# A decode step (attention over a cache, mixed with a gated feed-forward): VectorE's eight groups as a hardware loop, and the result stored over two queues

## The chip, the cores and the metric

The kernel runs on one core of a Trainium2 chip. The metric is the device time of one execution in microseconds (us). A core has TensorE (PE, matrix products), VectorE (DVE), ScalarE (ACT), GpSimd (POOL) and SyncE (SP), each with its own instruction stream, and sixteen DMA engines that all of them share. The streams are tied together by semaphores only: an instruction waits until a semaphore has reached a value, and raises one when it is done.

## What is computed

One token attends to a cache of 32768 positions with 32 query heads and 8 key/value heads, and the result is mixed with a gated feed-forward of the same token.

```python
g = sigmoid((x * gate_w).sum(-1, keepdims=True))
q = (x @ wq) as 32 heads of 128
k, v = the caches, each of 8 heads used by 4 query heads
p = softmax(q . k / sqrt(128), over 32768 positions)
a = (p @ v) as one row of 4096, @ wo           # 4096 x 512
b = (silu(x @ w_gate) * (x @ w_up)) @ w_down   # 512 -> 1792 -> 512
out = g * a + (1 - g) * b                      # 1 x 1 x 512, bf16
```

Each cache has 8 x 32768 x 128 bf16 numbers, 67 MB. Every number of the caches and weights is read once, 148.1 MB in all, and the output is 1 KB.

## The kernel before, in words

**Groups and pages.** A group (`G` = 8) is one key/value head with its four query heads (`HPG`). Its 32768 positions come in two halves (`NB` = 2) of 16384, and one half of K or of V is a page: 128 partitions x 32 KB, 4.19 MB. There are five page buffers: two for K (`PG_K`), two for V (`PG_V`; one of them first holds the gate and up weights) and one that first holds `wq` and later `wo`.

**Loads.** All large loads are issued by SP, in one order written out by hand: `wq`, gate, up, the first K and V pages, then K and V pages in turn, and at the end `wo` in five pieces with `w_down` between (lines 291 to 319). A K page's buffer is loaded again when PE has made the last transposition from it (`sem_fill`, in `load_k`), a V page's when PE's products on it are done (`sem_v_free`). SP issues in order: a load that waits holds up those behind it.

**A K page.** PE transposes it 1024 positions at a time (eight transpositions, line 387, into one of two PSUM buffers `pst`); VectorE copies that to SBUF (`ktT`, four buffers, line 667); PE multiplies the copy by the group's queries (`qcur`, line 399) into `ps_sc`. There are eight such units per page (`UPP`). PE runs two units ahead (`LAG`): its transpositions into a `pst` buffer wait for the copy two units back (`sem_cp`). After each page VectorE takes the maximum over it (line 672), and after both pages the maximum of the two (line 674). GpSimd takes that over the partitions, ScalarE turns it into a bias and computes the exponentials (line 545).

**A V page.** PE multiplies the exponentials with it (line 443). The sums stand in strips of partitions; ScalarE copies them out (`acc`, line 557), and four small products (`emit_reduce`, line 425) gather them in a few columns of `ps_m`, which VectorE copies to `oT` (`copy_red`, line 658).

**Loops.** PE's stream is a hardware loop already: `pe.Fori(0, (G + 1) * STEP, STEP)`, in which turn g does the K pages of group g and the V pages of group g - 1. Its waits compare semaphores with the loop's register `i` plus a constant, which is why several semaphores advance by `STEP` = 16 per group. VectorE, ScalarE, GpSimd and SP have the eight groups written out, each with constant wait values.

**The end.** After the last group VectorE adds the exponentials' sums, takes their reciprocals, scales `oT` (line 695) and transposes it; PE multiplies by `w_down` and `wo`, the first 18 pieces of `wo` as wide rows, the other 14 as four strips (line 466). VectorE copies the four strips to `res_row` (line 705), in partitions 0, 32, 64 and 96. SP, which waits for that (`sem_dve_row`), stores the four rows of 128 with one DMA (line 322) and waits for its completion.

Of the kernel before, what the change touches and what calls it, by code (L numbers as in the profile page):

```python
# [6 lines left out]
ALU = mybir.AluOpType  # L7
AX = mybir.AxisListType
# [5 lines left out]
def bass_gated_mix__gqa_block_cached__swiglu_ffn__decode_kernel(  # L14
# [18 lines left out]
    HPG = H // G  # L33
# [22 lines left out]
    SCALE = float(DH) ** -0.5  # L56
    assert UPG == STEP and UPP % NKT == 0 and UPP % NST == 0
    assert KC * H * DH <= PAGE and 2 * KC * F <= PAGE and WOJ * NOUT <= PAGE
# [15 lines left out]
    with ExitStack() as es:  # L74
# [53 lines left out]
        def T(name, shape, dt):  # L128
            return es.enter_context(nc.sbuf_tensor(name, shape, dt))
# [21 lines left out]
        qT = T("qT", [128, H], BF16)  # L151
        qblk = T("qblk", [128, G, 2, 2 * HPG], BF16)
        qcur = T("qcur", [128, 2, 2 * HPG], BF16)
# [6 lines left out]
        ET = T("ET", [128, NT, HPG], BF16)  # L160
        pmaxf = T("pmaxf", [128, G * NB, HPG], FP32)
        pmax = T("pmax", [128, G, HPG], FP32)
        gmax = T("gmax", [128, G, HPG], FP32)
# [4 lines left out]
        acc = T("acc", [128, RQ, DH], FP32)  # L168
        oT = T("oT", [128, H], FP32)
        rS = T("rS", [128, H], FP32)  # L170
# [30 lines left out]
        wgu = page[:, PG_F, 0 : 2 * KC * F].rearrange("p (w c f) -> p w c f", w=2, c=KC)  # L201
        wo_v = page[:, PG_X, 0 : WOJ * NOUT].rearrange("p (j n) -> p j n", j=WOJ)

        with nc.Block("main") as block:
            @block.gpsimd
            def _(pool):
# [58 lines left out]
                for g in range(G):  # L265
                    pool.wait_ge(sem_pmax, 3 * (g + 1))
                    pool.partition_all_reduce(  # L267
                        gmax[:, g, :], pmax[:, g, :], 128, ReduceOp.max
                    ).then_inc(sem_gmax, 1)

            @block.sync
            def _(sp):
# [46 lines left out]
                for k in range(1, len(sem_wo)):  # L319
                    load_wo(k)  # L320
                sp.wait_ge(sem_dve_row, 1)
                sp.dma_start(
                    out[0, 0, :].rearrange("(c n) -> c n", c=OC),
                    res_row[0 : 32 * (OC - 1) + 1 : 32, :],
                ).then_inc(sem_out, 16)
                sp.wait_ge(sem_out, 16)

            @block.tensor
            def _(pe):
# [78 lines left out]
                def emit_k(i, b):  # L408
                    pe.wait_ge(sem_page[PG_K[b]], i + 16)
                    for u in range(UPP + LAG):  # L410
                        if u >= LAG:
                            pe.wait_ge(sem_cp, i + (UPP * b + u - LAG + 1))
                        if u < UPP:
                            emit_fill(b, u)
                        if u >= LAG:
                            if u == LAG:
                                pe.wait_ge(sem_exp, i + 8 * (b + 1))
                            ins = emit_scores(b, u - LAG)
                    ins.then_inc(sem_sc, 1)

                def emit_reduce(i):
                    pe.wait_ge(sem_acc, i)
                    pe.wait_ge(sem_rc, i)
                    for q in range(RQ):
                        ins = pe.matmul(  # L425
                            ps_m[:, M_P0 : M_P0 + HPG],
                            acc[:, q, :],
                            sel4[:, q * HPG : (q + 1) * HPG],
                            start=(q == 0),
                            stop=(q == RQ - 1),  # L430
                        )
                    ins.then_inc(sem_red, 1)

# [89 lines left out]
            def _(act):  # L523
# [30 lines left out]
                def emit_acc(g):  # L554
                    act.wait_ge(sem_v_free, NB * (g + 1))
                    act.wait_ge(sem_red, g + 1)
                    act.activation(  # L557
                        acc[:, :, :].rearrange("p q d -> p (q d)"), ps_o[:, :], ACT.Copy
                    ).then_inc(sem_acc, STEP)

                for g in range(G):
                    emit_exps(g)
                    if g:
                        emit_acc(g - 1)
                emit_acc(G - 1)

            @block.vector
            def _(dve):
# [7 lines left out]
                dve.memset(acc[:, :, :], 0.0).then_inc(sem_acc, STEP)  # L576
                dchain(dve.memset(qblk[:, :, :, :], 0.0))
                dve.sem_inc(sem_rc, 2 * STEP)
# [44 lines left out]
                for par in range(2):  # L623
                    lo, hi = 64 * par, 64 * (par + 1)
                    dchain(
                        dve.tensor_copy(
                            qblk[lo:hi, :, :, par * HPG : (par + 1) * HPG],
                            ps_o[lo:hi, 0 : 2 * H].rearrange(
                                "p (e g h) -> p g e h", e=2, h=HPG
                            ),  # L630
                        )
                    )
                dve.tensor_copy(qcur[:, :, :], qblk[:, 0, :, :])
                dve.memset(ps_o[:, :], 0.0).then_inc(sem_ps0, 1)
# [20 lines left out]

                def copy_red(g):
                    dve.wait_ge(sem_red, g + 2)
                    dve.tensor_copy(
                        oT[:, g * HPG : (g + 1) * HPG], ps_m[:, M_P0 : M_P0 + HPG]
                    ).then_inc(sem_rc, STEP)  # L660

                for g in range(G):
                    for b in range(NB):
                        f = NB * g + b
                        for u in range(UPP):
                            dve.wait_ge(sem_fill, UPP * f + u + 1)
                            dve.tensor_copy(  # L667
                                ktT[:, u % NKT, :], pst[u % NST][:, :].bitcast(BF16)
                            ).then_inc(sem_cp, 1)
                        dve.wait_ge(sem_sc, f + 1)  # L670
                        sc = ps_sc[b][:, :].rearrange("p (t h) -> p h t", h=HPG)
                        dve.tensor_reduce(pmaxf[:, f, :], sc, AX.X, ALU.max).then_inc(sem_pmax, 1)  # L672
                    dve.wait_ge(sem_pmax, 3 * g + 2)
                    dve.tensor_tensor(  # L674
                        pmax[:, g, :], pmaxf[:, f - 1, :], pmaxf[:, f, :], ALU.max
                    ).then_inc(sem_pmax, 1)
                    if g + 1 < G:
                        dve.tensor_copy(qcur[:, :, :], qblk[:, g + 1, :, :])
                    if g >= 2:
                        copy_red(g - 2)  # L680

# [4 lines left out]
                dve.memset(ps_w[:, :], 0.0).then_inc(sem_psw, 1)  # L686
                copy_red(G - 2)
                dve.wait_ge(sem_pe_S, 1)
# [3 lines left out]
                )  # L692
                copy_red(G - 1)
                dve.wait_ge(sem_rc, STEP * (G + 2))
                dve.tensor_tensor(oTs[:, :], oT[:, :], rSg[:, :], ALU.mult).then_inc(
                    sem_dve_oT1, 1
                )
                dve.wait_ge(sem_dve_oT1, 1)
# [35 lines left out]
```

## Time and profile before

| | |
|---|---|
| time, median of 3 runs | 354.7 us (354.43 to 354.92) |
| the profiled execution's own time | 353.97 us |
| its span (first to last instruction) | 352.2 us |
| PE busy | 266.7 us (76%) |
| VectorE busy, 203 instructions | 177.5 us (50%) |
| ScalarE busy | 32.3 us (9%) |
| GpSimd busy | 5.8 us (2%) |
| DMA | 148.24 MB, mean 421 GB/s |
| mean granted PE clock | 0.849 |

The profile is of one execution. Its page gives each engine's busy time, the span cut into 40 slices with the busy share of each in tenths, the DMA queues, and groups of instructions: line, engine, operation, output<-input with sizes, count, then busy time and mean duration, and after the bar the idle time in front of them and what ended it. A chain of waits follows the work that ended last back from the end, each piece with its start and length. Other answers of the trace are a timeline (start, duration, instruction) and windows (busy time per engine in a stretch with counts, then granted clock, DMA share and GB/s). "SPq" and "ACTq" are the DMA issues of SP and ACT. "issue" is time in which an engine waited for nothing that the profile shows. What lies between the span and the execution's time is before the first or after the last instruction.

### The profile page before, as it was taken

Reading aid. Unit: us, or ns where it says so; the run is one execution under the profiler, and the core shown is the slowest. Engines: PE = TensorE matmul, PEld = TensorE weight load, DVE = VectorE, ACT = ScalarE, POOL = GpSimd, SP = SyncE. Lnnn points to the kernel's source line nnn. Section 1 sums busy time; section 2 is a strip of 40 time slices with the busy share of each in tenths; the row PEclk is TensorE's granted clock in tenths of the full one; section 3 lists DMA queues with packets and bytes.
Section 4 is the critical chain, followed back from the end, with each engine's and each line's share of the span. In section 5 each row is a group of like instructions: output and inputs, shape, how many; then the busy total and the mean of one; then the engine's idle time right before and its main releaser. Section 6 shows DMA issues by size and latency. Waiting matters only on the chain.

```text
span 352.2 us, 8737 instructions
## 1 busy us (share of the span) xinstructions
PE 266.7 (76%) x4005; PEld 227.3 (65%) x4005; DVE 177.5 (50%) x203; ACT 32.3 (9%) x148; POOL 5.8 (2%) x24
## 2 busy tenths in 40 slices
PE   0446996998999959796897969794987849794365
PEld 0436986967796939494886849492967749492122
DVE  0311877644783929275473819183654719292001
ACT  1000000400030040003000040004000120004000
POOL 0200000000000000000000000000000000000000
PEclk9999989876998989679696969789698969899565
DMA  8999999999999999999999999999999999999994
GB/s 328 411 443 422 437 437 423 419 424 447 435 421 424 447 436 417 424 443 443 417 424 435 447 421 424 435 443 424 424 435 443 424 421 435 443 424 412 426 425 170
DMA packets 5925, 148.24 MB, mean 421 GB/s; under 512 B 666, under 2 KB 668, under 8 KB 924
## 3 DMA queue, kind: packets, MB, share of 16 engines
q1 hardware_dynamic: 5912, 148.12, 98.2%
q8 instruction: 6, 0.10, 0.1%
q14 instruction: 3, 0.02, 0.0%
q10 hardware_dynamic: 4, 0.00, 0.0%
HBM read 148.11 MB, written 0.00 MB: 421 GB/s over the span
## 4 chain that ended last, share of the span: by engine, by line
DMA 62%; PE 33%; DVE 3%; SPq 1%; issue 0%
DMA page<-in_A_k_cache_dram 55%; PE pst L387 24%; DMA page<-in_A_wo_dram 7%; PE ps_sc L399 6%; DVE ktT L667 3%; PE ps_o L443 2%; PE pst L466 1%; PE ps_m L425 0%; SPq L293 0%; SPq L310 0%; SPq L316 0%; SPq L291 0%; SPq L274 0%; DVE res_row L705 0%
## 5 line engine op out<-in xcount | busy, mean ns | idle before, releaser
L667 DVE COPY ktT<-pst 128x2048 bf16<-128x2048 bf16 x128 | 155.8, 1224 | 108.5 <-PE pst L387 101.4
L387 PE MATMUL pst<-ident_f,page 128*128 128x128 f32 x1024 | 156.1, 309 | 40.7 <-DMA page<-in_A_k_cache_dram 38.9
L387 PEld LDWEIGHTS pst<-ident_f,page 128*128 128x128 f32 x1024 | 132.5, 160 | 52.2 <-DMA page<-in_A_k_cache_dram 46.9
L399 PE MATMUL ps_sc<-qcur,ktT 128*128 128x8 bf16 x2048 | 67.8, 166 | 8.6 <-DVE ktT L667 8.6
L399 PEld LDWEIGHTS ps_sc<-qcur,ktT 128*128 128x128 bf16 x2048 | 66.9, 97 | 11.3 <-DVE ktT L667 10.0
L443 PE MATMUL ps_o<-page,ET 128*16 128x512 bf16 x512 | 44.3, 507 | 10.0 <-DMA page<-in_A_v_cache_dram 10.0
L443 PEld LDWEIGHTS ps_o<-page,ET 128*16 128x16 bf16 x512 | 13.7, 107 | 30.2 <-issue 24.5
L536 ACT ACTIVATE nbias<-gmax 128x4 f32<-128x4 f32 x8 | 1.7, 206 | 262.1 <-POOL gmax L267 262.1
L545 ACT ACTIVATE ET<-ps_sc,nbias 128x128 bf16<-128x128 f32 x64 | 24.1, 553 | 0.7
L545 ACT ACTIVATION_READ_ACCUMULATOR ET<-ps_sc,nbias 128x1 f32 x64 | 18.0, 282 | 0.0
L672 DVE TENSOR_REDUCE pmaxf<-ps_sc 128x4 f32<-128x512 f32 x16 | 11.1, 692 | 10.4 <-PE ps_sc L399 10.4
L425 PE MATMUL ps_m<-sel,acc 128*128 128x4 f32 x72 | 10.4, 268 | 3.7 <-ACT acc L557 3.7
L425 PEld LDWEIGHTS ps_m<-sel,acc 128*128 128x128 f32 x72 | 9.8, 211 | 4.4 <-ACT acc L557 4.4
L372 PE MATMUL ps_m<-xT,page 128*128 128x1 bf16 x112 | 6.9, 198 | 5.2 <-DMA page<-in_B_w_up_dram 5.2
L372 PEld LDWEIGHTS ps_m<-xT,page 128*128 128x128 bf16 x112 | 6.8, 159 | 5.3 <-DMA page<-in_B_w_up_dram 5.3
L689 DVE RECIPROCAL rS<-pst 128x32 f32<-128x32 f32 x1 | 0.4, 358 | 17.3 <-PE pst L478 17.3
L267 POOL PARTITION_ALL_REDUCE gmax<-pmax x8 | 3.0, 374 | 292.3 <-DVE pmax L674 292.3
L348 PE MATMUL ps_m<-xT,page 128*128 128x1 bf16 x128 | 3.5, 165 | 4.8 <-DMA page<-in_A_wq_dram 4.8
L557 ACT ACTIVATE acc<-ps_o 128x512 f32<-128x512 f32 x8 | 5.2, 648 | 18.3 <-PE ps_o L443 18.3
L348 PEld LDWEIGHTS ps_m<-xT,page 128*128 128x128 bf16 x128 | 3.5, 104 | 4.8 <-issue 4.8
L335 PE MATMUL ps_m<-ones_bf,x_row 1*128 1x1 bf16 x4 | 0.3, 172 | 8.3 <-DMA gw_row<-in_gate_w_dram 8.3
L335 PEld LDWEIGHTS ps_m<-ones_bf,x_row 1*128 1x128 bf16 x4 | 0.2, 114 | 8.3 <-DMA gw_row<-in_gate_w_dram 8.3
(68 smaller groups left out, 27.6 us busy)
## 6 DMA issues: line engine op xcount, KB each, us to landing
page<-in_A_k_cache_dram SPq DMA_DIRECT2D x16, 4096.0 KB, 27.6
page<-in_A_v_cache_dram SPq DMA_DIRECT2D x16, 4096.0 KB, 31.2
page<-in_A_wq_dram SPq DMA_DIRECT2D x1, 4096.0 KB, 12.6
page<-in_A_wo_dram SPq DMA_DIRECT2D x2, 1024.0 KB, 24.8
page<-in_B_w_gate_dram SPq DMA_DIRECT2D x1, 1792.0 KB, 16.5
page<-in_B_w_up_dram SPq DMA_DIRECT2D x1, 1792.0 KB, 21.2
wd<-in_B_w_down_dram SPq DMA_DIRECT2D x1, 1792.0 KB, 21.7
page<-in_A_wo_dram SPq DMA_DIRECT2D x1, 1280.0 KB, 24.3
```

Of the source, the lines that this page charges most:

```text
L267: pool.partition_all_reduce(gmax[:, g, :], pmax[:, g, :], 128, ReduceOp.max).then_inc(sem_gmax, 1)
L348: ins = pe.matmul(ps_m[:, M_Q0 + h : M_Q0 + h + 1], wq_v[:, c, h * DH : (h + 1) * DH], xT[:, c : c + 1], start=(c == 0), stop=(c == KC - 1),)
L372: ins = pe.matmul(ps_m[:, base + j : base + j + 1], wgu[:, w, c, :].rearrange("d (p j) -> d j p", j=FC)[:, j, :], xT[:, c : c + 1], start= ...
L387: ins = pe.transpose(pst[u % NST][:, k * 128 : (k + 1) * 128], kv[:, n * 128 : (n + 1) * 128], ident_f[:, :],)
L399: ins = pe.matmul(ps_sc[b][:, col : col + 2 * HPG], kt[:, k, e, :], qcur[:, e, :], start=(e == 0), stop=(e == 1),)
L425: ins = pe.matmul(ps_m[:, M_P0 : M_P0 + HPG], acc[:, q, :], sel4[:, q * HPG : (q + 1) * HPG], start=(q == 0), stop=(q == RQ - 1),)
L443: ins = pe.matmul(ps_o[32 * c : 32 * c + RQ * HPG, :], ET[:, n : n + RQ, :].rearrange("p n h -> p (n h)"), view[:, k * RQ : (k + 1) * RQ, ...
L466: ins = pe.matmul(ps_c[32 * oc : 32 * oc + 1, 0:128], lhs, rhs[:, oc * 128 : (oc + 1) * 128], start=first, stop=last, skip_group_check=True,)
L545: act.activation(ET[:, b * R : (b + 1) * R, h], sc[:, h, :], ACT.Exp, bias=nbias[:, g, h : h + 1], scale=SCALE, accum_out=esum[:, g, b, h ...
L557: act.activation(acc[:, :, :].rearrange("p q d -> p (q d)"), ps_o[:, :], ACT.Copy).then_inc(sem_acc, STEP)
L667: dve.tensor_copy(ktT[:, u % NKT, :], pst[u % NST][:, :].bitcast(BF16)).then_inc(sem_cp, 1)
L672: dve.tensor_reduce(pmaxf[:, f, :], sc, AX.X, ALU.max).then_inc(sem_pmax, 1)
```

## The change

VectorE's eight groups become one body in a hardware loop whose register `i` runs from 0 in steps of 16. Its waits use `i` plus a constant. The semaphores that VectorE waits for or raises in the loop now advance by 16 per group (`sem_sc` by 8 per page, `sem_pmax` by 4 + 4 + 8, `sem_red` by 16), and PE, ScalarE and GpSimd follow suit in their values. Tiles that are addressed by group are addressed by `i`: `pmax` and `oT` get 16 columns per group of which 4 are used, `oT` with two unused groups in front; `qblk` becomes flat, with two more groups that stay zero, since the copy to `qcur` now also runs after the last group. `pmaxf` has two rows per turn instead of sixteen in all. The copy of the reduced row, which the first two groups don't have, stands behind a test of the register. The store of the result becomes two DMAs of two rows, one issued by SP and one by ScalarE, and SP waits for both.

```diff
-        qblk = T("qblk", [128, G, 2, 2 * HPG], BF16)
+        qblk = T("qblk", [128, (G + 2) * STEP], BF16)
-        pmaxf = T("pmaxf", [128, G * NB, HPG], FP32)
-        pmax = T("pmax", [128, G, HPG], FP32)
+        pmaxf = T("pmaxf", [128, NB, HPG], FP32)
+        pmax = T("pmax", [128, (G + 1) * STEP], FP32)
-        oT = T("oT", [128, H], FP32)
+        oT = T("oT", [128, (G + 2) * STEP], FP32)
...
+        def store(eng, k):
+            eng.dma_start(
+                out[0, 0, 256 * k : 256 * (k + 1)].rearrange("(c n) -> c n", c=2),
+                res_row[64 * k : 64 * k + 33 : 32, :],
+            ).then_inc(sem_out, 16)
...
                 sp.wait_ge(sem_dve_row, 1)
-                sp.dma_start(
-                    out[0, 0, :].rearrange("(c n) -> c n", c=OC),
-                    res_row[0 : 32 * (OC - 1) + 1 : 32, :],
-                ).then_inc(sem_out, 16)
-                sp.wait_ge(sem_out, 16)
+                store(sp, 0)
+                sp.wait_ge(sem_out, 32)
...
                 emit_acc(G - 1)
+                act.wait_ge(sem_dve_row, 1)
+                store(act, 1)
...
-                def copy_red(g):
-                    dve.wait_ge(sem_red, g + 2)
-                    dve.tensor_copy(
-                        oT[:, g * HPG : (g + 1) * HPG], ps_m[:, M_P0 : M_P0 + HPG]
-                    ).then_inc(sem_rc, STEP)
-
-                for g in range(G):
+                def copy_red(i, at):
+                    dve.wait_ge(sem_red, i)
+                    dve.tensor_copy(oT[:, at], ps_m[:, M_P0 : M_P0 + HPG]).then_inc(sem_rc, STEP)
+
+                with dve.Fori(0, G * STEP, STEP) as i:
                     for b in range(NB):
-                        f = NB * g + b
                         for u in range(UPP):
-                            dve.wait_ge(sem_fill, UPP * f + u + 1)
+                            dve.wait_ge(sem_fill, i + (UPP * b + u + 1))
                             dve.tensor_copy(
                                 ktT[:, u % NKT, :], pst[u % NST][:, :].bitcast(BF16)
                             ).then_inc(sem_cp, 1)
-                        dve.wait_ge(sem_sc, f + 1)
+                        dve.wait_ge(sem_sc, i + 8 * (b + 1))
                         sc = ps_sc[b][:, :].rearrange("p (t h) -> p h t", h=HPG)
-                        dve.tensor_reduce(pmaxf[:, f, :], sc, AX.X, ALU.max).then_inc(sem_pmax, 1)
-                    dve.wait_ge(sem_pmax, 3 * g + 2)
+                        dve.tensor_reduce(pmaxf[:, b, :], sc, AX.X, ALU.max).then_inc(sem_pmax, 4)
+                    dve.wait_ge(sem_pmax, i + 8)
                     dve.tensor_tensor(
-                        pmax[:, g, :], pmaxf[:, f - 1, :], pmaxf[:, f, :], ALU.max
-                    ).then_inc(sem_pmax, 1)
-                    if g + 1 < G:
-                        dve.tensor_copy(qcur[:, :, :], qblk[:, g + 1, :, :])
-                    if g >= 2:
-                        copy_red(g - 2)
+                        pmax[:, bass.ds(i, HPG)], pmaxf[:, 0, :], pmaxf[:, 1, :], ALU.max
+                    ).then_inc(sem_pmax, 8)
+                    dve.tensor_copy(
+                        qcur[:, :, :].rearrange("p e n -> p (e n)"), qblk[:, bass.ds(i + STEP, STEP)]
+                    )
+                    with dve.If(i > STEP):
+                        copy_red(i, bass.ds(i, HPG))
...
-                copy_red(G - 2)
+                copy_red(G * STEP, slice(G * STEP, G * STEP + HPG))
...
-                copy_red(G - 1)
+                copy_red((G + 1) * STEP, slice((G + 1) * STEP, (G + 1) * STEP + HPG))
                 dve.wait_ge(sem_rc, STEP * (G + 2))
-                dve.tensor_tensor(oTs[:, :], oT[:, :], rSg[:, :], ALU.mult).then_inc(
-                    sem_dve_oT1, 1
-                )
+                dve.tensor_tensor(
+                    oTs[:, :].rearrange("p (g h) -> p g h", h=HPG),
+                    oT[:, 2 * STEP :].rearrange("p (g s) -> p g s", s=STEP)[:, :, 0:HPG],
+                    rSg[:, :].rearrange("p (g h) -> p g h", h=HPG),
+                    ALU.mult,
+                ).then_inc(sem_dve_oT1, 1)
```

## The prediction, on record before the run

> **What bounds the kernel now.** I read the slices and queues first, to see whether any resource is full from end to end.
>
> ```profile
> DVE  0311877644783929275473819183654719292001
> DMA  8999999999999999999999999999999999999994
> GB/s 328 411 443 422 437 437 423 419 424 447 435 421 424 447 436 417 424 443 443 417 424 435 447 421 424 435 443 424 424 435 443 424 421 435 443 424 412 426 425 170
> q1 hardware_dynamic: 5912, 148.12, 98.2%
> q8 instruction: 6, 0.10, 0.1%
> q14 instruction: 3, 0.02, 0.0%
> ```
>
> The DMA engines are busy in every slice but the first and last; the loads alone take 98.2% of sixteen engines' span. VectorE (DVE) is busy half of the time. So the end is set by 148.12 MB at the DMA rate, with a start and a tail around it. Second, the chain of waits, for what lies after the last byte:
>
> ```profile
> 277.42 28.47 DMA page<-in_A_k_cache_dram
> ...
> 319.76 0.33 SPq L274
> ...
> 321.08 26.38 DMA page<-in_A_wo_dram
> 347.46 0.04 issue
> 347.50 1.88 PE pst L466 x56
> 349.38 0.03 issue
> 349.41 0.41 PE pst L466 x7
> 349.82 0.02 issue
> 349.85 0.29 DVE res_row L705
> ```
>
> A K page lands 28.47 us after its issue, although 4.19 MB at 431 GB/s (the windows row of 122 to 320 us) are 9.7 us: 18.7 us of other loads lie ahead of it. The last 4.7 us (347.50 to 352.19) are final row products, result copy and store. Third, how far SP runs ahead, because a slower VectorE can only matter by delaying the semaphores that release SP's loads. The windows give what had been moved at three issues:
>
> ```profile
> 0.00:44.40 44.40, 22.83 (x402) 22.46 (x403) 13.74 (x34) 1.67 (x3) 2.82 (x16) 1.00 0.97 409
> 0.00:92.75 92.75, 65.06 (x1018) 60.95 (x1019) 45.28 (x63) 6.16 (x21) 3.21 (x17) 0.91 0.99 419
> 0.00:319.76 319.76, 251.66 (x3826) 220.80 (x3826) 174.30 (x192) 28.49 (x131) 5.81 (x24) 0.87 1.00 428
> ```
>
> The last column is GB/s. At 44.40 us (SP's K load after the first page's last transpose), 20.45 MB had been issued (wq and three pages of 4.19 MB, two weights of 1.835 MB) and 44.40 x 409 = 18.16 MB moved: 2.29 MB, or 5.3 us at 431 GB/s, were still queued. At 92.75 us: 41.42 issued, 38.86 moved, 5.9 us left. At 319.76 us: 148.12 less the 9.18 MB issued from there on (V page 4.19, wd 1.84, rest of wo 3.15) is 138.94; 136.86 moved; 4.8 us left. Between 122 and 320 us the queue is deeper, as the 28.47 us show. These three are the thinnest covers.
>
> **The change part by part.**
>
> *Same work, looped.* The eight groups keep their 128 copies, 16 reduces and 8 maxima; one more qcur copy runs after the last group. It takes 0.17 us (row of L678) and lies before a VectorE idle of 3.73 us (until ScalarE's exponentials are done, 322.61). The semaphore steps are rescaled to match on PE, ACT and POOL, with no instruction more or less there: 0. The larger qblk memset (112 ns for 64 columns, 80 now) lies in the first 9 us, before VectorE's 7.30 us wait for PE: 0.
>
> *Register waits.* Before every K copy but the first there is now a register add, since its wait compares with the loop counter plus a constant: 15 to 16 adds a turn. The copies stand here:
>
> ```profile
> L667 DVE COPY ktT<-pst 128x2048 bf16<-128x2048 bf16 x128 | 155.8, 1224 | 108.5 <-PE pst L387 101.4
> 46.25 0.29 issue
> ```
>
> No register add on VectorE is in the trace. Lower bound of its price: 0, because PE already does the same adds between its groups (one before each transposition group of eight), and its chain alternates 0.93 us of L387 with 0.38 us of L399 without a gap. Upper bound: 0.29 us, PE's issue time at 46.25 where it passes the boundary of a K part, branches and an add together. I take 0.03 us: a sequencer can work on the next add while the copy of 1.224 us runs. VectorE's eight copies take 10.20 us, a period of (10.20 - 1.22)/7 = 1.28 us, against PE's 0.93 + 0.38 = 1.31 us per unit, so 0.03 us is all free room there is; any more than that goes into the page's time. What is late next is the last transposition of the page, then SP's K load, then the DMA queue if it runs dry. Up to 92.75 us there are 32 copies. PE waited for DMA in front of two of those pages (2.55 us before 61.92, 1.68 us before 81.38), so lateness is eaten by 4.2 us there. The queue goes dry only if 32d > 4.2 + 5.9, d = 0.32 us per copy. At 44.40 us eight copies give d = 0.66; at 319.76 us the last page waited for its own data at 305.88, so 8d > 4.8, d = 0.60. Even the upper bound of 0.29 us stays below 0.32. Cost: 0; without that cover it would be 128 x 0.03 = 4 us.
>
> *Loop, branch, addresses.* Each turn adds about five control instructions: two for register addresses, the test for the reduced row, the counter add and the branch back. At 0 to 0.29 us each that is 0 to 1.5 us a turn. They stand behind the second reduce, where VectorE waits for PE's next transposes anyway: 3.55 us at 63.93, 1.88 us at 97.49 (the shortest), 4.74 to 8.21 later. The wait for s_pmax now holds the address instruction; behind it are the maximum, the qcur copy, the row copy and the branch. GpSimd's maximum, then the exponentials, then PE's next scores wait for them. In the last group the maximum ends at 318.80 and the V page that needs the exponentials lands only at 325.46; exponentials end at 322.57, so 2.9 us cover it. Cost 0 at either bound.
>
> *Code loading.* The trace has nine instruction packets in the span, while PE's own loop makes nine turns of over 400 matmuls; a loop that loaded its body on every turn could not do with nine. All of them are 0.12 MB, 0.3 us at 431 GB/s, which bounds the gain from a shorter VectorE program: 0 to -0.3 us. I take -0.05, the 0.02 MB of q14. The Trainium skill (Runtime: NRT & Kernel Launch, Instruction fetch mechanics) speaks against the change: a taken branch whose target lies outside the two resident blocks waits for a fetch, and so kernels prefer full unrolling. With the roughly 2 us that DMA: Bandwidth & Descriptors gives as a transfer's fixed cost, eight turns would be an estimate of 16 us of VectorE idle, of which only the excess over each turn's cover could reach the end; the packet count above says the body stays resident.
>
> *Store.* It is on the path:
>
> ```profile
> 0.72 0.51 ACTq L524 DMA_DIRECT2D x_row<-in_A_x_dram  x1
> 1.27 0.21 ACTq L525 DMA_DIRECT2D gw_row<-in_gate_w_dram  x1
> 350.17 0.63 SPq L322 DMA_DIRECT2D out_dram<-res_row  x1
> SPq L204 <- DMA out_dram<-res_row: 1.0, 1, 1.0
> ```
>
> The columns are start, duration, queue and line; the last row is SP's wait. One issue of four rows takes 0.63 us, and 1.0 us more to completion. After, SP and ACT are released by the same semaphore and issue two rows each side by side. ACT has nothing else left (its last copy ends at 341.95). If the shorter transfer issues like SP's page loads (0.33 us), the gain is 0.30 us; if ACT's issue comes wholly behind SP's at its own 0.21 to 0.63 us, the loss is up to 0.63. ACT's first issue took 0.51, its second 0.21, so two issues overlapped are nearest to 0.5 to 0.63: I take 0.
>
> *Tail on VectorE.* Output scaling reads a strided oT of the same 128x32 size (0.19 us). It feeds the wide products, which end at 346.51, and the partial row at 347.25, while the next products wait for wo data until 347.50 and the partial row is used from 348.20: 0.9 us of cover. Cost 0 unless the tile read goes over five times slower.
>
> **Sum.** Span 352.2 + 0 (waits) + 0 (loop) - 0.05 (code) + 0 (store) = 352.15 us. Around the span lie 353.97 - 352.19 = 1.78 us, giving 353.9 for a run like the profiled one. The median of 354.7 is 0.73 us above that execution, so 354.65, written 354.7. The bounds of the unknown parts are -0.3 - 0.3 = -0.6 and +0.63: 354.1 to 355.3. A measurement of this kernel tells about 0.2% (0.71 us) from no change, and its three runs spread over 0.49 us.
>
> **Rivals.**
>
> *Slower: register waits empty the load queue.* Place: the copies of the first four K pages, where PE and VectorE paced each other and the queue held 5 to 6 us. It decides from 0.32 us per copy. At 0.5 us, 32 x 0.5 - 10.1 = 5.9 us of idle DMA engines, and 360.6 us in all. For it: only 0.03 us of room in a unit. Against: it needs more than the largest control price in the trace, sixteen times in a row. Chance 0.09.
>
> *Slower: the two stores follow each other.* If ACT's store starts only when SP's is through (0.63 + 1.0 us), the end is 1.6 us later: 356.3. For it: ACT has issued nothing for 349 us, and the kernel now ends with the later of two. Against: the two queues have no semaphore between them. Chance 0.08.
>
> *Faster: the stream itself gets shorter.* The rate is 431 GB/s between 122 and 320 us, but 409 up to 44.40. If VectorE's code packets cost more than their bytes, and the store gains 0.3, it is 0.3 + 0.3 + some 0.3 = 0.9 us: 353.8. For it: the slower early stretch. Against: q14 is three packets. Chance 0.10.
>
> *The split does nothing.* If the store's time is in its completion alone, the result is the forecast's; it is counted there.
>
> **How the numbers follow.** Forecast (covered everywhere) 0.73; rivals 0.09, 0.08, 0.10. Faster 0.10, same 0.73, slower 0.17. The range goes from 354.0, just outside the lower bound, to 356.3, which takes in the serial stores; left out are the emptied queue (0.09) and most of the faster case (0.09). The likeliest case alone spans 354.1 to 355.3.
>
> **What would show it.** DMA busy 9 in all middle slices and 431 GB/s from 122 to 320 us: waits covered. A copy group of eight at 10.2 to 10.5 us: adds hidden; over 12.8 us (0.32 x 8 more): the first rival. Idle before the first copy of each turn still put down to PE: loop covered. No more than nine instruction packets: body resident. The last result copy within 0.3 us of 349.85, and from its end to the span's end 2.05 us before: over 3 us means the second rival. A span that moves with DMA idle, or an end that is not the store, would make the prediction wrong.

## The result, and the profile after

The changed kernel takes 353.89 us (median of 13 runs, 353.25 to 354.30) against 354.56 us for before in the same comparison (13 runs, 354.15 to 355.00). The ratio is 0.998, with a 95% interval from 0.9972 to 0.9989: faster by 0.2%, which is small, but the interval leaves out 1. The forecast was 354.7 us and no measurable change, with a range from 354.0; the result lies 0.1 us below that range.

The first rows are those shown of before: VectorE's and the DMA engines' slices and three of the DMA queues, from the changed kernel's page. The profiled execution took 353.30 us with a span of 351.5 us (before: 353.97 and 352.2).

```profile
DVE  0311958565692938266563818283655628183011
DMA  8999999999999999999999999999999999999995
q1 hardware_dynamic: 5908, 148.11, 98.4%
q8 instruction: 6, 0.10, 0.1%
q14 instruction: 2, 0.02, 0.0%
```

The loads bound it as before. One line differs: q14 had three instruction packets, and has two. The chain of waits at the end (start, length, what):

```profile
276.27 28.75 DMA page<-in_A_k_cache_dram
...
346.59 0.04 issue
346.64 1.88 PE pst L469 x53
348.51 0.03 issue
348.54 0.41 PE pst L469 x8
348.95 0.02 issue
348.97 0.29 DVE res_row L713
```

Piece for piece it is the chain of before, 0.87 us earlier: the last products start at 346.64 where they started at 347.50, and the result copy at 348.97 where it started at 349.85. So the gain was made in the loads, and some of it is lost behind the copy, in the store. The timeline shows its two issues (start, length, queue), and SP's waits its completion (total, times, longest):

```profile
349.29 0.60 SPq L205 DMA_DIRECT2D out_dram<-res_row  x1
349.30 0.58 ACTq L205 DMA_DIRECT2D out_dram<-res_row  x1
```

```profile
SPq L210 <- DMA out_dram<-res_row: 1.2, 1, 1.2
```

The two issues do run side by side, but one of two rows takes 0.60 us where one of four took 0.63, and the wait behind it is 1.2 us instead of 1.0. From the end of the result copy to the end of the span it is 351.5 - 349.26 = 2.24 us against 352.19 - 350.14 = 2.05.

VectorE's copies as a group, and from the timeline the boundary of two groups:

```profile
L671 DVE COPY ktT<-pst 128x2048 bf16<-128x2048 bf16 x128 | 155.9, 1224 | 106.0 <-PE pst L390 98.9
```

```profile
82.59 10.20 DVE L671 COPY ktT<-pst 128x2048 bf16<-128x2048 bf16 x8 [5.58 <-PE pst L390]
93.50 0.69 DVE L676 TENSOR_REDUCE pmaxf<-ps_sc 128x4 f32<-128x512 f32 x1 [0.72 <-PE ps_sc L402]
94.33 0.16 DVE L678 TENSOR_TENSOR pmax<-pmaxf 128x4 f32 x1
94.44 0.17 DVE L681 COPY qcur<-qblk 128x16 bf16 x1
96.29 10.20 DVE L671 COPY ktT<-pst 128x2048 bf16<-128x2048 bf16 x8 [1.68 <-PE pst L390]
```

A copy takes 1224 ns and eight of them 10.20 us, both as before: the register adds are hidden. The same boundary before:

```profile
94.63 0.69 DVE L672 TENSOR_REDUCE pmaxf<-ps_sc 128x4 f32<-128x512 f32 x1 [0.65 <-PE ps_sc L399]
95.36 0.16 DVE L674 TENSOR_TENSOR pmax<-pmaxf 128x4 f32<-128x4 f32 x1
```

The wait in front of a reduce grew from 0.65 to 0.72 us, and between the reduce and the maximum there are 0.14 us (94.33 - 94.19) where there were 0.04. The idle time before the next group is still put down to PE.

**Where the load time went.** The loads have the same bytes and the same sum of packet times in both traces (345.63 and 345.65 us per engine, from the start, length and size of each packet), yet the last byte lands at 349.26 us before and at 348.38 us after. (Times of packets are counted here and below so that the first load packet starts at 2.10 us in every run; on the span's own clock, which the fences use, they are 0.33 to 0.37 us smaller.) The sixteen engines don't finish together, and the kernel waits for the last. Each engine has the same series of packet sizes, so the trace's packets can be strung into sixteen series by size and by start behind the end of the one before. Two engines that run in step can be taken for each other, but the sixteen end times hold. Sorted, in us:

```
before   346.4 346.5 346.7 346.8 346.8 346.9 347.2 347.2 348.0 348.1 348.1 348.2 348.2 348.2 348.3 349.26
changed  346.5 346.6 346.6 346.7 346.8 346.9 347.4 347.7 348.0 348.0 348.1 348.1 348.2 348.2 348.4 348.38
```

(The last two of the changed kernel are 348.35 and 348.38.) Six engines end near 346.5, some at 348 or a little more, and in before one is a microsecond behind all others. The packets between the loads explain the steps: a 16 KB instruction packet (q8, all between 19 and 66 us) stands about 1.0 us in an engine's line, and the load packet behind it mostly takes some 0.5 us longer than the usual 1.22 us; an 8 KB one (q14) stands 0.3 us and lengthens the next by 0.25 to 0.65 us. Before had 8 KB packets at 59.5, 131.4 and 285.4 us, the changed kernel at 59.7 and 131.3. The one at 285.4 us stood 0.33 us, and the load packet that starts at its end took 1.87 us: 0.98 us for that engine, and the last engine ends 0.95 us behind the next. So the first theory (F in the expectations): the packet at 285.4 us was VectorE's code, it fell on an engine that was late already, and the shorter program doesn't need it. The trace doesn't name a packet's engine, so that it was the late one is argued from the end times.

### The profile page after: what moved, and what is told of

Read it like the earlier page. It is cut to its first block, busy times and chain, and to the rows that moved or that the text cites. A ratio compares the mean times of both kernels' runs of the same rounds, so it can differ in the third digit from the quotient of the medians.

```text
span 351.5 us, 8924 instructions
## 1 busy us (share of the span) xinstructions
PE 263.6 (75%) x4005; PEld 228.2 (65%) x4005; DVE 178.6 (51%) x204; ACT 32.1 (9%) x148; POOL 5.8 (2%) x24
## 4 chain that ended last, share of the span: by engine, by line
DMA 61%; PE 33%; DVE 3%; SPq 1%; issue 1%
DMA page<-in_A_k_cache_dram 54%; PE pst L390 24%; DMA page<-in_A_wo_dram 7%; PE ps_sc L402 6%; DVE ktT L671 3%; PE ps_o L446 2%; PE pst L469 1%; PE ps_m L428 0%; SPq L299 0%; SPq L316 0%; SPq L322 0%; SPq L297 0%; SPq L280 0%; DVE res_row L713 0%
## 5 line engine op out<-in xcount | busy, mean ns | idle before, releaser
L671 DVE COPY ktT<-pst 128x2048 bf16<-128x2048 bf16 x128 | 155.9, 1224 | 106.0 <-PE pst L390 98.9
L446 PE MATMUL ps_o<-page,ET 128*16 128x512 bf16 x512 | 40.5, 472 | 8.0 <-DMA page<-in_A_v_cache_dram 8.0
L428 PE MATMUL ps_m<-sel,acc 128*128 128x4 f32 x72 | 11.3, 280 | 3.9 <-ACT acc L560 3.9
L428 PEld LDWEIGHTS ps_m<-sel,acc 128*128 128x128 f32 x72 | 10.6, 226 | 4.5 <-ACT acc L560 4.5
```

The source lines that it names most:

```text
L428: ins = pe.matmul(ps_m[:, M_P0 : M_P0 + HPG], acc[:, q, :], sel4[:, q * HPG : (q + 1) * HPG], start=(q == 0), stop=(q == RQ - 1),)
L446: ins = pe.matmul(ps_o[32 * c : 32 * c + RQ * HPG, :], ET[:, n : n + RQ, :].rearrange("p n h -> p (n h)"), view[:, k * RQ : (k + 1) * RQ, ...
L671: dve.tensor_copy(ktT[:, u % NKT, :], pst[u % NST][:, :].bitcast(BF16)).then_inc(sem_cp, 1)
```

## The experiments

**The two halves of the change alone.** First the loop with the store of before:

```diff
-                store(sp, 0)
-                sp.wait_ge(sem_out, 32)
+                sp.dma_start(
+                    out[0, 0, :].rearrange("(c n) -> c n", c=OC),
+                    res_row[0 : 32 * (OC - 1) + 1 : 32, :],
+                ).then_inc(sem_out, 16)
+                sp.wait_ge(sem_out, 16)
...
-                act.wait_ge(sem_dve_row, 1)
-                store(act, 1)
```

> VectorE's loop as in the changed kernel, the store as before (one DMA of four rows from SP). Theory F (one code packet): in the trace of before an 8 KB code packet ran at 285.4 us on one DMA engine, held back the loads of that engine by about 1 us, and that engine was the last to finish its loads, at 349.26 us against 348.31 for the next; the looped program has no such packet. Under F this run has 2 code packets on q14, its last load byte lands near 348.4 us, and with the single store, which ended 1.69 us after the last result copy in before against 1.89 us for the split one, it takes 0.9 us less than before: 353.7 us, 0.2 us less than the changed kernel. Theory S (the split store gains 0.3 to 0.7 us, the loop nothing): 354.5 us, as before. Theory L (the loop gains by other pacing of VectorE, whatever the packets): 353.7 us too, so L and F are told apart by the padded run.

353.64 us, ratio 0.9976 (0.9967 to 0.9985). The end of its chain, then from the timeline its store, then SP's wait for it:

```profile
321.42 25.47 DMA page<-in_A_wo_dram
346.89 0.04 issue
346.94 1.88 PE pst L466 x54
...
349.28 0.29 DVE res_row L708
```

```profile
349.60 0.63 SPq L322 DMA_DIRECT2D out_dram<-res_row  x1
```

```profile
SPq L204 <- DMA out_dram<-res_row: 1.0, 1, 1.0
```

Two packets on q14, the last load byte at 348.69 us, and the store is as short as it was. The loop alone makes the gain. Then the split store with VectorE's groups written out:

```diff
-                sp.dma_start(
-                    out[0, 0, :].rearrange("(c n) -> c n", c=OC),
-                    res_row[0 : 32 * (OC - 1) + 1 : 32, :],
-                ).then_inc(sem_out, 16)
-                sp.wait_ge(sem_out, 16)
+                store(sp, 0)
+                sp.wait_ge(sem_out, 32)
...
+                act.wait_ge(sem_dve_row, 1)
+                store(act, 1)
```

> VectorE's eight groups written out as before, the store split over SP and ACT as in the changed kernel. Theory F: the 8 KB code packet near 285 us is there (3 packets on q14), the last load byte lands near 349.3 us, and the split store adds 0.2 us: 354.75 us, 0.1 to 0.3 us above before. Theory S: 353.9 us, as the changed kernel. Theory L: as F.

354.78 us, ratio 1.001 (1.0001 to 1.0019): slower by 0.1%, three packets on q14, the last byte at 349.65 us. Theory S is out. F and L (the loop's pacing) are still together.

**Code length against looping.** Unused instructions in the looped program, in VectorE's idle time behind the loop:

```diff
+        pad = T("pad", [128, 256], FP32)
...
+                for j in range(123):
+                    dve.memset(pad[:, j : j + 1], 0.0)
                 dve.wait_ge(sem_pe_S, 1)
```

> The changed kernel with 123 memsets of one unused column each on VectorE, behind its loop where it idles from 325 to 340 us, so that its program has 220 instructions as before written out (97 in the changed kernel). They add about 123 x 0.07 = 8 us of VectorE time inside 15 us of idle. Theory F: the third code packet on q14 is back, at some time behind the early ones. If it falls on a DMA engine that has already been held back by a code packet, the time goes back up by about 0.7 to 0.9 us, to 354.7; if it falls on one that has not, that engine ends at 346.5 + 1 = 347.5 us, ahead of the last, and the time stays at 353.9. The packet count and the end of each engine's loads tell which. Theory L or S: no change, 353.9 us, wherever the packet falls.

354.91 us, ratio 1.0005 (0.9996 to 1.0014): the whole gain is gone, although loop and register waits are untouched. The last byte lands at 349.83 us, the next engine ends at 348.2. There are three packets on q14. Its queue, then its timeline:

```profile
q14 instruction: 3, 0.02, 0.0%
```

```profile
325.24 3.06 DVE L695 MEMSET pad<- 128x1 f32 x109
328.65 0.43 DVE L695 MEMSET pad<- 128x1 f32 x14 [0.36 <-issue]
342.46 0.36 DVE L697 RECIPROCAL rS<-pst 128x32 f32<-128x32 f32 x1 [13.38 <-PE pst L482]
```

The memsets took under 4 us and were done at 329.1, 13 us before VectorE was needed; they can't have delayed anything themselves. The third packet ran at 332.2 us: after VectorE had passed a block's end (the 0.36 us pause behind the 109th memset), another block was fetched, although the 26 instructions that were left fit into the block just entered. With half as many, and with twice as many:

> The changed kernel with 60 unused one-column memsets behind VectorE's loop: 157 instructions in its program instead of 97 (220 in before, 220 in the run with 123 memsets). In the earlier runs the third 8 KB packet on q14 came when VectorE was at about its 170th to 186th instruction. Theory F: no third packet here, and the time of the changed kernel, 353.9 us. Theory P (the memsets themselves, or the VectorE time that they take, made the run with 123 of them slower): 354.3 to 354.5 us, half of the way, with two packets.

> The changed kernel with 251 unused one-column memsets behind VectorE's loop: 348 instructions. They take some 17 us, from 325 us to 342 us, so that they may just reach the reciprocals at 340 us; of that, up to 2 us could show at the end if the products with wo come late. Theory F: 4 packets on q14, one more engine held back for 0.7 to 1 us: 354.9 to 355.5 us, with the last load byte at or behind that of the run with 123. Theory P: 355.0 us or more with the last load byte near 348.4 us, so the end of the loads tells the two apart.

With 60: 353.57 us, ratio 0.9972 (0.9960 to 0.9984), two packets, as fast as the changed kernel. With 251: 355.45 us, ratio 1.0025 (1.0016 to 1.0034), four packets, last byte at 350.23 us while the next engine ends at 348.4. Theory P is out: 60 memsets cost nothing. From the run with 251, its queue, then its timeline:

```profile
q14 instruction: 4, 0.03, 0.0%
```

```profile
325.42 3.06 DVE L695 MEMSET pad<- 128x1 f32 x109
328.83 3.64 DVE L695 MEMSET pad<- 128x1 f32 x128 [0.35 <-issue]
334.38 0.42 DVE L695 MEMSET pad<- 128x1 f32 x14 [1.91 <-issue]
```

Pauses lie 128 instructions apart, so 8 KB is a block of 128. At the second one VectorE stood for 1.91 us; the third packet had run just then, at 332.8 us, so it was waiting for code that came through the loaded DMA engines.

The end times agree. In the five profiles with a third packet the last engine ends 0.95 to 1.8 us behind the next; in the seven with two packets it is 0.03 to 0.54 us, in the one with a single packet (ScalarE's loop, below) 0.75. That the packet hits the late engine five times of five looks like more than chance; how an engine is chosen for a packet is not in the traces and was not tried.

**The loop itself.** Four groups, then two, in the loop's body:

```diff
-                with dve.Fori(0, G * STEP, STEP) as i:
-                    for b in range(NB):
+                with dve.Fori(0, G * STEP, NG * STEP) as i:
+                    for h in range(NG):
+                        o = h * STEP
+                        for b in range(NB):
...
-                            dve.wait_ge(sem_fill, i + (UPP * b + u + 1))
+                                dve.wait_ge(sem_fill, i + (o + UPP * b + u + 1))
```

> The changed kernel with four groups in the loop's body and two turns, so that VectorE's program is about as long as before written out, but has the register waits of the changed kernel (128 copies that each wait on the register). pmax, qblk and oT are three groups wider. Theory F: VectorE's code is again longer than what is resident at the start, so at least one more 8 KB packet on q14 in the span than the changed kernel's 2, and perhaps more if the jump back fetches again; 353.9 to 354.8 us depending on which DMA engine it falls on. Theory L (register waits and loop pacing make the gain): 353.9 us, with the same end of loads whatever the packets.

> The changed kernel with two groups in the loop's body and four turns: 141 VectorE instructions instead of 97. Theory F: still short of the point at which the third 8 KB packet came (170 to 186 instructions), so 2 packets on q14 and the time of the changed kernel, 353.9 us, where four groups in the body gave 354.55 us with 3 packets. If a longer body by itself costs time (theory U), 354.1 to 354.3 us with 2 packets.

Four groups (225 instructions): three packets, 354.55 us, ratio 1.000 (0.999 to 1.001). Two groups (141): two packets, 353.40 us, ratio 0.9965 (0.9953 to 0.9978). Both have all the register waits, and one has the gain and the other none of it: theory L is out, and so is U. The third packet of the run with four groups came at 161.4 us, while the first turn was in its fourth group. It came once, not in each turn: the body, most of those 225 instructions, stayed resident across the jump back.

**The store.** VectorE's loop with all four rows stored by ScalarE (the edit is against the loop with SP's single store):

```diff
-                sp.wait_ge(sem_dve_row, 1)
-                sp.dma_start(
-                    out[0, 0, :].rearrange("(c n) -> c n", c=OC),
-                    res_row[0 : 32 * (OC - 1) + 1 : 32, :],
-                ).then_inc(sem_out, 16)
                 sp.wait_ge(sem_out, 16)
...
+                act.wait_ge(sem_dve_row, 1)
+                act.dma_start(
+                    out[0, 0, :].rearrange("(c n) -> c n", c=OC),
+                    res_row[0 : 32 * (OC - 1) + 1 : 32, :],
+                ).then_inc(sem_out, 16)
```

> VectorE's loop, and the whole result (four rows) stored by one DMA from ScalarE; SP only waits for it. In the changed kernel both issues took 0.6 us side by side, but ScalarE's two rows moved 0.27 us after SP's. If that is ScalarE's queue (theory A), this store ends 0.2 to 0.3 us later than SP's single one: 353.85 us, as the changed kernel. If it is the splitting, with both issues at the same time (theory B), it ends as SP's single one: 353.6 us.

353.43 us, ratio 0.9961 (0.9948 to 0.9975). Its issue and the copy before it:

```profile
349.67 0.29 DVE L708 CAST res_row<-pst 128x128 bf16<-128x128 f32 x1 [0.98 <-PE pst L461]
349.99 0.60 ACTq L562 DMA_DIRECT2D out_dram<-res_row  x1
```

The copy ends at 349.96 and the span at 352.0: 2.04 us, as for SP's single store (2.05). So ScalarE's queue is no slower, and theory B holds: it is the two stores issued together that cost 0.2 us more than one. In the five profiles with one store the span ends 2.04 to 2.06 us behind the result copy, in the eight with two 2.24 to 2.26. In the changed kernel the second pair of rows moves 0.27 us behind the first, though the issues coincide; what puts them in line was not tried.

The changed kernel and the loop with one store, once more on one chip:

> The changed kernel, beside the loop with the single store on the same chip: 353.9 us.

> The loop with the single store from SP once more: 0.2 to 0.3 us less than the changed kernel in this call, 353.65 us, since its store ends 0.2 us sooner after the last copy.

353.77 us (11 runs, ratio 0.9977, 0.9968 to 0.9986) and 353.23 us (5 runs, ratio 0.9962, 0.9949 to 0.9976). The loop with the single store has the lower median both times, by 0.25 us in the first two runs, which were not made side by side, and by 0.54 in this pair. The intervals overlap, and two groups in the body with the split store (353.40) came as low on this chip, so the medians alone don't show it: the 0.2 us rest on the traces.

**More loops.** ScalarE's groups as a loop, then PE's early products too:

```diff
+                with act.Fori(0, G * STEP, STEP) as i:
+                    act.wait_ge(sem_gmax, i + STEP)
...
+                                accum_out=esum[:, bass.ds(i + (4 * b + h), 1)],
```

> VectorE's loop, the single store, and ScalarE's eight groups as a hardware loop too (gmax, esum by register, one nbias; 180 ScalarE instructions become about 60). Theory F: one or both of the two 8 KB packets left on q14 (59 and 132 us) are ScalarE's and go, which takes away one or two of eight chances that two packets meet on one engine: 353.2 to 353.6 us, never slower than the loop alone (353.64). Theory R (register waits cost, here on the exponentials' path): 353.7 to 354.2 us.

353.62 us, ratio 0.9971 (0.9960 to 0.9982), against 353.64 for VectorE's loop alone. One packet is left on q14, that at 58 us; the one at 131 us was ScalarE's. It made no difference, which fits a packet that fell on an engine other than the last, but the trace doesn't name the engine. So not every block that is saved gains, and why this one didn't is open. The expected price of register waits (theory R) did not show either, but something else did, in the groups of this run:

```profile
L548 ACT ACT_TABLE_LOAD x8 | 10.3, 1283 | 256.2 <-POOL gmax L267 256.2
```

The table load for the exponential, one before the groups when they are written out, is now in the body and runs in each turn, 1.28 us each. ScalarE's idle time hides it.

```diff
-                for h in range(H):
+                with pe.Fori(0, H, 1) as h:
...
-                            ps_m[:, M_Q0 + h : M_Q0 + h + 1],
+                            ps_m[:, bass.ds(h + M_Q0, 1)],
```

> As the run with ScalarE's loop, and PE's 128 products with wq and 112 with gate and up as hardware loops of four and eight products a turn; the loop turns cost PE up to 0.3 us each in the first 32 us, up to 10 us for 46 turns, in front of loads that land at 12 and 24 us. Theory F: PE's program loses some 460 instructions, so one or two of the six 16 KB packets on q8 go; since one packet on an otherwise free engine is enough to end at 348.1 us, the last load byte stays near 348.2 us and the time within 0.3 us of the run with ScalarE's loop. Theory T (the total of code bytes sets the loss): 0.1 us less per 16 KB at 431 GB/s over sixteen engines, no more than 0.1 us. If the loop turns use up the cover of 5 us that the early load queue has, 1 us or more slower.

387.25 us, ratio 1.0912 (1.0897 to 1.0927): outside both theories, and far beyond the "1 us or more" that was named for loop turns that use up the cover. Its GB/s by slice, then from the timeline PE in the first of those loops:

```profile
GB/s 326 426 438 434 430 61 0 2 225 426 430 335 424 434 434 434 430 434 434 434 434 434 434 430 434 434 434 430 434 434 427 434 427 420 420 434 426 438 414 166
```

```profile
14.06 0.58 PE L352 MATMUL ps_m<-xT,page 128*128 128x1 bf16 x4 [5.21 <-DMA page<-in_A_wq_dram]
15.11 0.56 PE L352 MATMUL ps_m<-xT,page 128*128 128x1 bf16 x4 [0.47 <-issue]
```

A turn of four products takes 1.01 us in the mean, where 128 of them written out took 3.55 us, 0.11 us for four: 0.9 us more for each turn, three times the price expected. K's first page had landed long before PE came to it at 68.5 us, SP had no buffer to load into, and the load queue ran dry for about three slices of 9.7 us. One 16 KB packet fewer on q8 can't be read against that.

**All runs together.** VectorE's instructions are counted in the built program. The runs are from more than one chip; each ratio is to before on the same one, and the row of before is that of the first comparison.

```
run                          VectorE  store  q14      last load   median   ratio to
                             instr.          packets  byte, us    us       before
before                         220    one    3        349.26      354.56   -
loop + split (changed)          97    two    2        348.38      353.89   0.9980
the same again                  97    two    2        348.80      353.77   0.9977
loop, one store (SP)            97    one    2        348.69      353.64   0.9976
the same again                  97    one    2        349.00      353.23   0.9962
loop, one store (ACT)           97    one    2        348.81      353.43   0.9961
two groups in the body         141    two    2        348.27      353.40   0.9965
60 unused                      157    two    2        348.85      353.57   0.9972
written out, split             220    two    3        349.65      354.78   1.0010
123 unused                     220    two    3        349.83      354.91   1.0005
four groups in the body        225    two    3        349.02      354.55   1.0000
251 unused                     348    two    4        350.23      355.45   1.0025
VectorE and ScalarE loops       97    one    1        349.08      353.62   0.9971
PE's early products too         97    one    1        383.52      387.25   1.0912
```

With the split store, four runs of three programs with two packets have medians of 353.40 to 353.89 and three programs with three packets 354.55 to 354.91: 1.1 us between the means (353.66 and 354.75), with or without a loop. In their profiles the last byte is 0.9 us apart in the mean (348.58 and 349.50). It is of one execution each and ranges over 0.7 us among all runs with two packets; that of the four groups, 349.02, is from the fastest of its executions.

## Why the prediction was wrong

- **Code loading, the step that failed.** The prediction bounded the gain from a shorter program by "0.12 MB, 0.3 us at 431 GB/s" and took 0.05. That spreads a packet's bytes over all sixteen engines. One engine carries the whole packet, and everything in its line waits; each load is cut over all sixteen and has landed when the slowest is through. The one packet that the loop saves cost about 1 us of the end, against 0.02 us of bytes. The packet itself showed it: 0.33 us in its engine's line and 0.65 us more for the load packet behind. The page's own line, "q14 instruction: 3, 0.02, 0.0%", invites this error, since its share is a mean over engines.
- **Passing a block.** The Trainium skill (Runtime: NRT & Kernel Launch, Instruction fetch mechanics) calls the cost of passing a code block, of 16 KiB there and 8 KB for VectorE here, mostly hidden. For VectorE that agrees with the 0.36 us pause; for the kernel it does not: three programs that pass one more block are 1.1 us slower.
- **The body stays resident.** Right: two packets in the looped program, none per turn, and only one more in all for the body of four groups.
- **Register waits.** Right at 0: copies of 1224 ns, eight in 10.20 us. With three packets and the split store on both sides, four groups with register waits took 354.55 us and the written-out groups without them 354.78.
- **Loop, branch, addresses.** Right at 0 on the path. The 0.1 us added in front of the maximum lies under the cover named. (The 4.74 us listed there is a wait inside a group; between later groups VectorE waits 6.34 to 8.21 us.)
- **Store.** Taken as 0 with bounds from -0.30 to +0.63; measured +0.2, by the wait for completion and not by the issue, which is as long for two rows as for four.
- **The faster rival** had the right sign and nearly the time (353.8, chance 0.10), and the right suspect in one of its three parts: code packets that cost more than their bytes. But 0.3 of its 0.9 us were a gain from the store, which cost 0.2, and it looked for the loss in the slower early stretch, while the packet that is saved ran at 285 us. That its time came so near is partly luck.
- **The slower rival of the emptied queue** didn't occur on VectorE. PE's loops show what it looks like when it does.
- **Range.** Its lower end, 354.0, took at most 0.3 us for code and 0.3 us for the store. The loop alone gained 0.85 us and the split cost 0.2, so the end was too high by the error on code.

One part of the path to the end was not in the prediction. In six of the profiles (written out with the split store, 123 unused, the store by ScalarE, the second run of the single store, two groups, ScalarE's loop) the chain doesn't end on wo but on the products, through the last V page. This is the run with 123:

```profile
320.50 17.65 DMA page<-in_A_v_cache_dram
...
346.45 0.20 DVE O L712
346.65 0.04 issue
346.70 1.98 PE pst L459 x16
348.67 1.86 PE pst L470 x53
350.53 0.02 issue
350.56 0.29 DVE res_row L716
```

The stretch from PE's first product on the last V page (338.27 us here) to VectorE's copy of the transposed row (346.45) takes 8.18 to 8.19 us in all six, where it took 6.51 before and 6.11 in the changed kernel. PE's granted clock, the last number but two of a windows row, tells them apart; before, changed and 123:

```profile
341.00:345.00 4.00, 3.32 (x37) 1.77 (x37) 1.36 (x6) 0.60 (x1) 0.00 (x0) 0.93 0.99 413
341.00:345.00 4.00, 3.30 (x41) 1.39 (x40) 0.78 (x6) 0.00 (x0) 0.00 (x0) 1.00 0.99 412
341.00:345.00 4.00, 3.82 (x28) 2.52 (x22) 0.95 (x4) 0.60 (x1) 0.00 (x0) 0.50 0.98 409
```

It is 0.50 in all six, and 0.82 to 1.00 in the five profiles with the shorter stretch. (The runs with four groups and with 251 also have 0.50, but end on their late loads.) So the 0.9 us of cover that the prediction gave to the tail's products is gone at the lower clock. On the span's own clock the result copy starts 0.94 to 0.95 us behind the last load byte in the five profiles and 1.07 to 1.58 us in the six: 0.1 to 0.6 us of a single execution that are not code loading (0.1 with 123 unused, 0.6 with the written-out split store, whose profiled execution is its slowest). Four of the six have one or two packets and medians of 353.23 to 353.62 us, so the clock is not what separates two packets from three. What lowers it was not found. A late V page is not needed: with two groups PE took it up at 336.71 us, earlier than in any other, and had 0.50.

## What to carry to other kernels

When the load stream sets the end, look at the engine that finishes last and not at the mean over sixteen: one small packet on one engine, a code fetch above all, can cost some fifty times its share of the bytes (here 1 us against 0.02). Count the instruction packets on the page before pricing a change in program length; in these runs a shorter VectorE program gained by a whole block or not at all, and a loop was one way to get it; a block less on ScalarE gained nothing. A loop's price depends on the engine and on how long a turn is: eight turns of some 30 us on VectorE cost nothing, and 46 turns of 1.0 to 1.5 us on PE cost 34 us.

## What the runs showed of the hardware that was not expected

- A code block of VectorE is 128 instructions (8 KB, pauses 128 memsets apart); another one is fetched after passing into a block, even with few instructions left, and one that was needed soon kept VectorE waiting for 1.91 us beside full load queues.
- An 8 KB code packet at 285.4 us stood 0.33 us in a DMA engine's line, and the load packet behind it took 1.87 us instead of 1.22.
- Two stores of two rows at once from two queues end 0.2 us later than one of four rows (2.24 to 2.26 us behind the result copy against 2.04 to 2.06); the issue takes 0.58 to 0.63 us in each case.
- In PE's loop four products whose output column comes from a register took 0.56 us (0.11 written out), and a turn had 0.43 to 0.47 us of issue besides.
- At a granted clock of 0.50 in 341 to 345 us the stretch from the last V page to the transposed row took 8.18 us, at 0.82 to 1.00 it took 6.11 to 6.51.
- A table load that stands once in front of written-out exponentials is repeated in each turn of a loop, at 1.28 us.
